# Retention and FFN in one kernel: w2's rows loaded ahead of the second pair of chunks, and the first tile's output blocks moved between those chunks' steps

## The chip, the cores and the metric

The kernel runs on one core of a Trainium2 chip. Its metric is the device time of one execution in microseconds (us). TensorE (PE) multiplies matrices into PSUM, VectorE (DVE), ScalarE (ACT) and GpSimd (POOL) do the elementwise work, and SyncE (SP) issues the DMAs that move data between HBM and SBUF. Each engine works through its own instructions in program order; semaphores order them among each other.

## The reference

Batch 4, 8 heads, 768 positions, head width 64; the FFN has 512 inputs and 1024 inner features. Inputs and output are float32.

```python
gamma = 1.0 - 2.0 ** (-5.0 - np.arange(H))
for t in range(S):
    state = gamma * state + outer(k[:, :, t], v[:, :, t])      # per batch and head, D x D
    y[:, :, t] = q[:, :, t] @ state / sqrt(D)
x = y.transpose(0, 2, 1, 3).reshape(B * S, H * D)              # 3072 x 512
out = (((x @ w1) * (x @ w2)) @ w3) @ w_out                     # 3072 x 512
```

## The kernel before

**Retention in chunks.** The sequence is cut into chunks of 128 positions, 6 for each of 4 batches, 24 in all. For chunk n the kernel casts q, k and v to 16 bits (v scaled by powers of gamma into the tile VP), transposes q and k, and then runs `scores(n)` (line 429: k times q into PSUM, masked by DVE into `am`, two operations at line 442), `kv(n)` (line 450: the update of the state; DVE adds at line 468 into `s`, POOL scales at line 469 into `t16`) and `outputs(n)` (line 472: v times `am` plus the state times q, and DVE scales the result into `XT` at line 485). `XT[m]` holds the transposed output of two chunks and is what the FFN reads.

**FFN by tiles.** w3 times w_out is multiplied once, at the start, into `W3O` (8 tiles). For each tile of up to 256 tokens an `a_unit` multiplies XT by w1 and ACT copies the result to `pa` (lines 515 to 518), a `b_unit` multiplies XT by w2 and DVE multiplies that with `pa` into `HT` (lines 520 to 527), and an `o_unit` multiplies 128 rows of HT by W3O, ACT evicts it with a scale, and SP stores it (lines 529 to 541). Tile 0 covers chunks 0 and 1, tile 1 chunk 2 alone, tile 2 chunk 3.

**The first tile is different.** Weights arrive by rows of 128, so `by_rows(W, ps, d)` (line 721) multiplies row block d of w1 or w2 into all eight output blocks, which fill four PSUM banks (`four_banks`, line 712). After four rows of w1 the banks are copied to SBUF (`pa`, held in two staging buffers), four rows of w2 follow, and DVE multiplies the two into `f0.HT` (lines 772 and 773). The rows are cast to 16 bits by ACT, DVE or POOL as they arrive.

**Chunks 0 to 3 are loaded in pairs** (`load_pair`, line 68): one DMA each for q, k and v of two chunks. In a pair's tiles half of each chunk lies on the wrong partitions, so `pair_casts` (line 303) is called twice for a chunk: once for the half that stays (POOL), once for the half that moves (DVE, or the engine that is named). It makes one cast of k, or two multiplications of v into VP, each over 64 partitions. `q_transposes(1, True)` transposes q of chunks 2 and 3 on PE and leaves the copies back to the caller (`q_back`). `transposes(n)` (line 406) transposes k on PE and writes two halves into KP, by ACT; for n = 2 DVE writes the second half (line 427).

**The order.** All of this is written out by hand: every engine runs its instructions in the order in which lines 645 to 779 call for them. The loads are issued at the start in the order of lines 133 to 145, on one queue, each into a free staging buffer; a DMA also waits for the eighth before it. From line 781 on a small queue of units (`fill`) feeds FFN work of tiles 1 and up between the steps of chunks 4 to 23 (`step`, line 600). In these steps `casts(n + 2)` (POOL), `dma_transposes(n + 2)` (line 385, two transposing DMAs on SP, from chunk 6 on) and `load_chunk(n + 4)` prepare the next chunks.

**Around the change.** Loads: row blocks of w1, then q and k of chunks 2 and 3, row 0 of w2, v, rows 1 to 3 of w2, then chunks 4 to 7. On PE, from line 730: rows 0 and 1 of w1, row 2, q transposes, part of row 3, k transposes of chunk 2, the rest of row 3, k transposes of chunk 3, scores(2), row 0 of w2, outputs(2), scores(3), row 1, kv(2), `a_unit(0)` of tile 1, row 2, `a_unit(2)`, row 3, `a_unit(4)`, outputs(3), `a_unit(6)`, kv(3), and the two output blocks of tile 0. The kernel is one function with nested helpers:

Of the kernel before, what the change touches and what calls it, by code (L numbers as in the profile page):

```python
# [12 lines left out]
MULT = mybir.AluOpType.mult  # L13
# [5 lines left out]
def kernel(  # L19
# [11 lines left out]
    nc = tc.nc  # L31
# [36 lines left out]
    def load_pair(m, names="qkv"):  # L68

        b, c = divmod(2 * m, NCH)  # L70
        for nm, src in (("q", q), ("k", k), ("v", v)):
            if nm not in names:
                continue
            if nm == "q":
                t = ld.tile([128, 2 * 512], FP, tag="q64", name="q64", bufs=3)
                q_in[m] = t
            else:
                t = new_stage()
                pair_in[nm, m] = t
            dma_in(  # L80
                t[:, :].rearrange("p (h x) -> p h x", x=2 * D),
                src[b, :, c * C : (c + 2) * C, :].rearrange("h (p t) d -> p h (t d)", t=2),
            )
# [26 lines left out]
    def load_rows(src, i):  # L110
        t = new_stage()
        dma_in(t[:, :], src[i * 128 : (i + 1) * 128, :])
        return t
# [23 lines left out]
    w3_st = {f: load_rows(moe_w3, f) for f in range(4, 8)}  # L137
    load_pair(0)
    w1_st = [load_rows(moe_w1, d) for d in range(4)]
    load_pair(1, "qk")  # L140
    w2_st = [load_rows(moe_w2, 0)]
    load_pair(1, "v")
    w2_st += [load_rows(moe_w2, d) for d in range(1, 4)]
    for n in range(4, 8):
        load_chunk(n)

# [64 lines left out]
    for h in range(H):  # L211
        p, r = h // 2, (h % 2) * 64
# [13 lines left out]
    def cast_to(dst, src, on_dve):  # L226
        if on_dve:
            nc.vector.tensor_copy(dst, src)  # L228
        else:
            nc.scalar.copy(dst, src)  # L230
# [72 lines left out]
    def pair_casts(n, moved, names="kv", eng=None):  # L303

        m, c = divmod(n, 2)
        rows = slice(c * 64, c * 64 + 64)
        t = 1 - c if moved else c
        to = slice(t * 64, t * 64 + 64)
        eng = eng or (nc.vector if moved else nc.gpsimd)
        if n not in k16s:  # L310
            k16s[n] = att.tile([128, 512], HP, tag="k16", name="k16", bufs=3)
        if "k" in names:
            (nc.scalar.copy if eng is nc.scalar else eng.tensor_copy)(
                k16s[n][to, :].rearrange("i (h d) -> i h d", d=D),
                pair_in["k", m][rows, :].rearrange("i (h t d) -> i h t d", t=2, d=D)[:, :, t, :],
            )
        for r in range(2 if "v" in names else 0):
            eng.tensor_tensor(  # L318
                VP[n % 3][to, :, r, r * 64 : r * 64 + 64],
                pair_in["v", m][rows, :].rearrange("j (p s t e) -> j p s t e", s=2, t=2, e=64)[:, :, r, t, :],  # L320
                VS2[rows, t, :].rearrange("j (p s) -> j p s", s=2)[:, :, r].unsqueeze(2).broadcast_to((64, NP, 64)),
                MULT,
            )
# [82 lines left out]
    def transposes(n, tag="psT"):  # L406
        if n >= NSTEP:
            return
        if by_dma(n):
            kT, kp = kTs.pop(n), KP[n % 2]  # L410
            nc.scalar.copy(kp[0:64, :, 0, :], kT[0:64, :, :])  # L411
            nc.scalar.copy(kp[64:128, :, 1, :], kT[64:128, :, :])  # L412
            return
        transposes_front(n, tag)
        transposes_back(n)

    def transposes_front(n, tag):
        k16 = k16s[n]
        ps = bank(tag, [128, NP, 128], HP, "psT")
        for p in range(NP):  # L420
            nc.tensor.transpose(ps[:, p, :], k16[:, p * 128 : (p + 1) * 128], ident16[:, :])
        kTs[n] = ps

    def transposes_back(n):
        kp, ps = KP[n % 2], kTs.pop(n)
        nc.scalar.copy(kp[0:64, :, 0, :], ps[0:64, :, :])
        cast_to(kp[64:128, :, 1, :], ps[64:128, :, :], n == 2)

    def scores(n, tags=("psA0", "psA1"), between=None):
        kp = KP[n % 2]  # L430
        am = att.tile([128, NP, 2, 128], HP, tag="am", name="am")
        for half in range(2):
            ps = bank(tags[half], [128, 2, 2, 128], FP, "psA")
            for i in range(2):
                p = half * 2 + i
                for r in range(2):
                    nc.tensor.matmul(  # L437
                        ps[:, i, r, :], lhsT=kp[:, p, r, :], rhs=queries(n, p), start=True, stop=True
                    )
            if half and between:  # L440
                between()
            nc.vector.tensor_tensor(  # L442
                am[:, half * 2 : half * 2 + 2, :, :].rearrange("j p s i -> j (p s) i"),
                ps[:, :, :, :].rearrange("j p s i -> j (p s) i"),
                (keep2 if n < 4 else keep)[:, :].unsqueeze(1).broadcast_to((128, 4, 128)),
                MULT,
            )
        ATs[n] = am

    def kv(n, tag="psK", eng=nc.gpsimd):  # L450
        k16, vp = k16s.pop(n), VP[n % 3]
        c = n % NCH
        if c == NCH - 1:
            return None
        ps = bank(tag, [128, NP, 128], FP, "psK")
        for p in range(NP):

            rhs = vp[:, p, :, :].rearrange("j s e -> j (s e)")
            rhs = bass.AP(rhs.tensor, rhs.offset, [list(rhs.ap[0]), [192, 2], [1, 64]])
            nc.tensor.matmul(  # L460
                ps[:, p, :], lhsT=k16[:, p * 128 : (p + 1) * 128], rhs=rhs, start=True, stop=True
            )
        t16 = att.tile([128, NP, 128], HP, tag="t16", name="t16")
        if c == 0:
            nc.vector.tensor_tensor(t16[:, :, :], ps[:, :, :], GS[:, :, :], MULT)
        else:
            s32 = att.tile([128, NP, 128], FP, tag="s32", name="s32")
            nc.vector.tensor_tensor(s32[:, :, :], ps[:, :, :], Tst[0][:, :, :], ADD)  # L468
            eng.tensor_tensor(t16[:, :, :], s32[:, :, :], GS[:, :, :], MULT)  # L469
        return t16  # L470
# [158 lines left out]
    def cast_w(W, st, d, on_dve):  # L629
        cast_to(W[d][:, :], st[d][:, :], on_dve)  # L630
# [81 lines left out]
    def four_banks(tags):  # L712
        got = []
        for t in tags:
            if t == "psF":
                got.append(ps_f.tile([128, 2, TB], FP, tag=t, name="psF"))
            else:
                got.append(bank(t, [128, 2, TB], FP, "psG"))
        return [t[:, :, :] for t in got]

    def by_rows(W, ps, d, cut=(0, TB), blocks=(0, 8)):
        cs = slice(*cut)
        for f in range(*blocks):
            nc.tensor.matmul(  # L724
                ps[f // 2][:, f % 2, cs], lhsT=W[d][:, f * 128 : (f + 1) * 128],
                rhs=XT[0][:, d, cs], start=(d == 0 and f % 2 == 0 and cut[0] == 0),
                stop=(d == 3 and f % 2 == 1),
            )
# [2 lines left out]
    by_rows(W1, ps, 0, (0, 128))  # L731
    by_rows(W1, ps, 0, (128, 256))
    by_rows(W1, ps, 1)
    for n in (2, 3):
        pair_casts(n, False, "k")
        pair_casts(n, True, "k", nc.scalar)
    by_rows(W1, ps, 2)
    q_back = q_transposes(1, True)
    q_back(0)
    q_back(1)  # L740
    by_rows(W1, ps, 3, blocks=(0, 3))
    transposes(2)
    by_rows(W1, ps, 3, blocks=(3, 8))
    transposes_front(3, "psK")
    pa = [hold[i // 2][:, i % 2 * 512 : i % 2 * 512 + 512].rearrange("p (a n) -> p a n", a=2) for i in range(4)]
    nc.gpsimd.tensor_copy(W2[0][:, :], w2_st[0][:, :])
    pair_casts(2, False, "v")
    pair_casts(3, False, "v")
    cast_to(pa[0], ps[0], False)
    cast_to(pa[1], ps[1], True)  # L750
    cast_to(pa[2], ps[2], False)
    scores(2, between=lambda: pair_casts(2, True, "v"))
    cast_to(pa[3], ps[3], True)
    transposes_back(3)
    cast_w(W2, w2_st, 1, False)
    cast_w(W2, w2_st, 2, False)
    cast_w(W2, w2_st, 3, False)
    ps = four_banks(("psF", "psF", "psF", "psT"))
    by_rows(W2, ps, 0)
    outputs(2, "psK")  # L760
    scores(3)
    by_rows(W2, ps, 1)
    t_new = kv(2, "psY")
    Tst[0] = t_new
    pair_casts(3, True, "v")
    f1 = ffn[1]
    f1.a_unit(0, "psK")
    by_rows(W2, ps, 2)
    f1.a_unit(2, "psA0")
    by_rows(W2, ps, 3)  # L770
    f1.a_unit(4, "psK")
    for i in range(4):
        nc.vector.tensor_tensor(f0.HT[:, 2 * i : 2 * i + 2, :], pa[i], ps[i], MULT)  # L773
    outputs(3, "psA1")
    f1.a_unit(6, "psA0")
    casts(4)
    Tst[0] = kv(3, "psK")
    f0.o_unit(0)
    f0.o_unit(1)

    for t in range(1, NT):
        late = ffn[t - 1].o_units() if t > 1 else []
# [49 lines left out]
```

## Time and profile before

| | us |
|---|---|
| median of 13 runs | 195.09 (194.71 to 196.02) |
| the profiled execution, its time | 195.44 |
| its span, first to last instruction | 193.5 |
| busy: PE / DVE / ACT / POOL | 184.4 / 117.9 / 99.3 / 85.4 |
| moved by DMA | 40.54 MB, 210 GB/s over the span |
| granted TensorE clock | 1.000 |

PE is busy for 95% of the span, so what matters is where it isn't: at the start, between 34 and 42 us, and at the end. In the rows of the profile each line gives the source line, the engine, the operation, the tile that is written and the tiles that are read; "L442 DVE ... am<-psA,keep" is the mask multiplication of the scores. In square brackets stands the time that the engine was idle before and the instruction or DMA that ended it. PEld is PE's weight load.

### The profile page before, as it was taken

What the parts mean: (1) busy time and instruction counts of PE and PEld (TensorE: products, weight loads), DVE (VectorE), ACT (ScalarE), POOL (GpSimd) and SP (SyncE); (2) the same over time, 40 slices, a digit from 0 to 9 for tenths busy, and PEclk for the clock granted to TensorE, in tenths of its full rate; (3) what the DMA queues carried; (4) which work ended last, traced back from release to release, by engine and by line L of the source; (5) the groups of instructions that cost most, each with busy time, mean ns of one, the idle gap of its engine ahead of it and who ended that gap; (6) DMA issues with size and microseconds to landing.
All of it is one profiled execution on the core that took longest, in us unless ns stands there. A gap on an engine that the chain in (4) does not pass through costs nothing.

```text
span 193.5 us, 4697 instructions
## 1 busy us (share of the span) xinstructions
PE 184.4 (95%) x1777; PEld 139.9 (72%) x1777; DVE 117.9 (61%) x220; ACT 99.3 (51%) x192; POOL 85.4 (44%) x146
## 2 busy tenths in 40 slices
PE   6799989879999999999999999999999999999993
PEld 2444657568797789777877787788778877887752
DVE  3227588599587768656665676575657665754220
ACT  6578455762445464455536453555455545533322
POOL 7600468638763747468152643862426432200000
PEclk9999999999999999999999999999999999999999
DMA  5999999998999989999999999969979931111004
GB/s 201 376 390 390 300 400 322 367 279 202 238 180 220 219 200 235 138 274 222 222 268 193 211 199 225 206 155 265 194 177 197 212 94 25 58 54 54 36 27 157
DMA packets 85030, 40.54 MB, mean 210 GB/s; under 512 B 61328, under 2 KB 80016, under 8 KB 85008
## 3 DMA queue, kind: packets, MB, share of 16 engines
q1 hardware_dynamic: 85008, 40.25, 87.9%
q8 instruction: 14, 0.23, 0.5%
q14 instruction: 8, 0.07, 0.2%
HBM read 29.36 MB, written 6.29 MB: 184 GB/s over the span
## 4 chain that ended last, share of the span: by engine, by line
PE 81%; DMA 10%; POOL 3%; DVE 2%; SPq 2%; issue 1%; ACT 1%; POOLq 0%; DVEq 0%
PE psF L508 39%; PE psO L534 21%; DMA stg<-in_v_dram 5%; PE psA L437 5%; DMA stg<-in_moe_w_dram 5%; PE psY L477 3%; PE psY L478 3%; PE psF L724 2%; PE psY L480 2%; PE psK L460 2%; POOL vp L318 2%; SPq L62 2%; PE psG L508 1%; PE psO L551 1%; DVE vp L318 1%
## 5 line engine op out<-in xcount | busy, mean ns | idle before, releaser
L508 PE MATMUL psF<-xt,w 128*128 128x256 f16 (+1 forms) x736 | 85.0, 266 | 0.0
L508 PEld LDWEIGHTS <-w 128*128 128x128 f16 x768 | 68.2, 98 | 7.2
L524 DVE TENSOR_TENSOR ht<-pa,psF 128x256 f16<-128x256 f32 x88 | 36.6, 417 | 22.5 <-PE psF L508 12.8
L518 ACT COPY pa<-psF 128x256 f32<-128x256 f32 x84 | 31.3, 372 | 33.8 <-PE psF L508 33.3
L442 DVE TENSOR_TENSOR am<-psA,keep 128x512 f16<-128x512 f32 x48 | 31.0, 685 | 21.0 <-PE psA L437 20.9
L534 PE MATMUL psO<-w3o,ht 128*128 128x512 f16 x184 | 43.3, 379 | 0.0
L469 POOL TENSOR_TENSOR t<-s,GS 128x512 f16<-128x512 f32 x15 | 19.3, 1284 | 37.5 <-DVE s L468 37.5
L539 ACT ACTIVATE osb<-psO 128x512 f32<-128x512 f32 x23 | 13.7, 597 | 37.0 <-PE psO L534 37.0
L534 PEld LDWEIGHTS <-ht 128*128 128x128 f16 x184 | 17.9, 98 | 16.9 <-DVE ht L773 0.2
L344 POOL TENSOR_TENSOR vp<-v,VS 128x256 f16<-128x256 f32 x40 | 23.8, 615 | 6.6 <-DMA v<-in_v_dram 2.5
L327 POOL CAST q<-q 128x1024 f16<-128x1024 f32 x12 | 12.6, 1053 | 27.3 <-DMA q<-in_q_dram 27.3
L485 DVE TENSOR_TENSOR xt<-psY,YS 128x512 f16<-128x512 f32 x24 | 17.8, 741 | 4.0 <-PE psY L480 3.6
L477 PE MATMUL psY<-am,vp 128*128 128x128 f16 x96 | 16.8, 219 | 1.0 <-POOL vp L318 0.8
L478 PE MATMUL psY<-am,vp 128*128 128x128 f16 x96 | 16.7, 219 | 0.6 <-DVE vp L318 0.6
L437 PEld LDWEIGHTS <-kp 128*128 128x128 f16 x192 | 12.5, 98 | 4.9 <-DVE kp L228 0.4
L340 POOL CAST k<-k 128x512 f16<-128x512 f32 x20 | 12.2, 611 | 5.2 <-PE psK L460 3.9
L468 DVE TENSOR_TENSOR s<-psK,t 128x512 f32<-128x512 f32 x16 | 11.0, 689 | 3.0 <-PE psK L460 2.7
L251 DVE COPY w3t<-psW 128x1024 f16<-128x1024 f16 x8 | 5.5, 690 | 10.0 <-PE psW L259 7.6
L437 PE MATMUL psA<-qTd,kp 128*128 128x128 f16 x144 | 11.1, 219 | 0.0
L411 ACT COPY kp<-kT 64x512 f16<-64x512 f16 x17 | 10.5, 618 | 0.8 <-DMA kT<-k 0.4
L480 PE MATMUL psY<-qTd,t 128*128 128x128 f16 x60 | 10.8, 219 | 0.0
L412 ACT COPY kp<-kT 64x512 f16<-64x512 f16 x17 | 10.5, 615 | 0.4
(82 smaller groups left out, 191.2 us busy)
## 6 DMA issues: line engine op xcount, KB each, us to landing
stg<-in_moe_w_dram SPq DMA_DIRECT2D x16, 512.0 KB, 8.3
q<-in_q_dram SPq DMA_DIRECT2D x12, 512.0 KB, 5.6
out_dram<-osb SPq DMA_DIRECT2D x23, 256.0 KB, 3.0
k<-in_k_dram SPq DMA_DIRECT2D x20, 256.0 KB, 5.3
v<-in_v_dram SPq DMA_DIRECT2D x20, 256.0 KB, 5.5
stg<-in_moe_w_out_dram SPq DMA_DIRECT2D x4, 512.0 KB, 7.2
stg<-in_k_dram SPq DMA_DIRECT2D x2, 512.0 KB, 11.0
stg<-in_v_dram SPq DMA_DIRECT2D x2, 512.0 KB, 8.5
```

Source lines behind the costliest of these rows:

```text
L344: nc.gpsimd.tensor_tensor(vp[:, :, r, r * 64 : r * 64 + 64], v32[:, :].rearrange("j (p s e) -> j p s e", s=2, e=64)[:, :, r, :], VS[:, :]. ...
L437: nc.tensor.matmul(ps[:, i, r, :], lhsT=kp[:, p, r, :], rhs=queries(n, p), start=True, stop=True)
L442: nc.vector.tensor_tensor(am[:, half * 2 : half * 2 + 2, :, :].rearrange("j p s i -> j (p s) i"), ps[:, :, :, :].rearrange("j p s i -> j ( ...
L469: eng.tensor_tensor(t16[:, :, :], s32[:, :, :], GS[:, :, :], MULT)
L477: nc.tensor.matmul(ps[:, p, :], lhsT=vp[:, p, 0, :], rhs=am[:, p, 0, :], start=True, stop=False)
L478: nc.tensor.matmul(ps[:, p, :], lhsT=vp[:, p, 1, :], rhs=am[:, p, 1, :], start=False, stop=(c == 0))
L480: nc.tensor.matmul(ps[:, p, :], lhsT=Tst[0][:, p, :], rhs=queries(n, p), start=False, stop=True)
L485: nc.vector.tensor_tensor(XT[n // 2][:, :, n % 2 * C : (n % 2 + 1) * C].rearrange("p a (i t) -> p a t i", t=2), ps[:, :, :].rearrange(orde ...
L508: nc.tensor.matmul(ps[:, i * w : (i + 1) * w], lhsT=W[d][:, (f + i) * 128 : (f + i + 1) * 128], rhs=XT[self.tok0 // TB][:, d, c0 : c0 + w] ...
L518: nc.scalar.copy(self.pa[f][:, :], ps[:, :])
L524: nc.vector.tensor_tensor(self.HT[:, f : f + TB // self.width, :].rearrange("p f n -> p (f n)"), self.pa.pop(f)[:, :], ps[:, :], MULT,)
L534: nc.tensor.matmul(psO[:, :], lhsT=self.HT[:, f, tb * 128 : (tb + 1) * 128], rhs=W3O[f][:, :], start=(f == 0), stop=(f == 7),)
```

## The change

The loads are reordered: all four rows of w2 come before the whole second pair. On PE the first tile now runs through: four rows of w1, four rows of w2, HT. The q transposes of chunks 2 and 3 follow, then the first output block of tile 0, the k transposes, and the second output block with scores(2) in its middle; then scores(3), kv(2), outputs(2), and the a units of tile 1 on PSUM banks of other names. The casts move along: w2's row 0 from POOL to ACT, row 3 from ACT to DVE; the moved half of v of chunk 2 goes ahead of its scores, that of chunk 3 ahead of scores(3). Instructions and their number on PE stay the same.

```diff
     load_pair(0)
     w1_st = [load_rows(moe_w1, d) for d in range(4)]
-    load_pair(1, "qk")
-    w2_st = [load_rows(moe_w2, 0)]
-    load_pair(1, "v")
-    w2_st += [load_rows(moe_w2, d) for d in range(1, 4)]
+    w2_st = [load_rows(moe_w2, d) for d in range(4)]
+    load_pair(1)
     for n in range(4, 8):
         load_chunk(n)
...
     by_rows(W1, ps, 1)
+    by_rows(W1, ps, 2)
+    by_rows(W1, ps, 3)
+    pa = [hold[i // 2][:, i % 2 * 512 : i % 2 * 512 + 512].rearrange("p (a n) -> p a n", a=2) for i in range(4)]
+    cast_w(W2, w2_st, 0, False)
+    cast_to(pa[0], ps[0], False)
+    cast_to(pa[1], ps[1], True)
+    cast_to(pa[2], ps[2], False)
+    cast_to(pa[3], ps[3], True)
+    cast_w(W2, w2_st, 1, False)
+    cast_w(W2, w2_st, 2, False)
+    cast_w(W2, w2_st, 3, True)
+    ps = four_banks(("psF", "psF", "psF", "psT"))
+    for d in range(4):
+        by_rows(W2, ps, d)
+    for i in range(4):
+        nc.vector.tensor_tensor(f0.HT[:, 2 * i : 2 * i + 2, :], pa[i], ps[i], MULT)
     for n in (2, 3):
         pair_casts(n, False, "k")
         pair_casts(n, True, "k", nc.scalar)
-    by_rows(W1, ps, 2)
     q_back = q_transposes(1, True)
     q_back(0)
     q_back(1)
-    by_rows(W1, ps, 3, blocks=(0, 3))
+    f0.o_unit(0)
     transposes(2)
-    by_rows(W1, ps, 3, blocks=(3, 8))
-    transposes_front(3, "psK")
-    pa = [hold[i // 2][:, i % 2 * 512 : i % 2 * 512 + 512].rearrange("p (a n) -> p a n", a=2) for i in range(4)]
-    nc.gpsimd.tensor_copy(W2[0][:, :], w2_st[0][:, :])
+    transposes(3, "psK")
     pair_casts(2, False, "v")
     pair_casts(3, False, "v")
-    cast_to(pa[0], ps[0], False)
-    cast_to(pa[1], ps[1], True)
-    cast_to(pa[2], ps[2], False)
-    scores(2, between=lambda: pair_casts(2, True, "v"))
-    cast_to(pa[3], ps[3], True)
-    transposes_back(3)
-    cast_w(W2, w2_st, 1, False)
-    cast_w(W2, w2_st, 2, False)
-    cast_w(W2, w2_st, 3, False)
-    ps = four_banks(("psF", "psF", "psF", "psT"))
-    by_rows(W2, ps, 0)
-    outputs(2, "psK")
-    scores(3)
-    by_rows(W2, ps, 1)
-    t_new = kv(2, "psY")
+    pair_casts(2, True, "v")
+    f0.o_unit(1, lambda: scores(2))
+    pair_casts(3, True, "v")
+    scores(3)
+    t_new = kv(2, "psY")
+    outputs(2, "psK")
     Tst[0] = t_new
-    pair_casts(3, True, "v")
     f1 = ffn[1]
-    f1.a_unit(0, "psK")
-    by_rows(W2, ps, 2)
-    f1.a_unit(2, "psA0")
-    by_rows(W2, ps, 3)
-    f1.a_unit(4, "psK")
-    for i in range(4):
-        nc.vector.tensor_tensor(f0.HT[:, 2 * i : 2 * i + 2, :], pa[i], ps[i], MULT)
+    f1.a_unit(0, "psT")
+    f1.a_unit(2)
+    f1.a_unit(4)
     outputs(3, "psA1")
     f1.a_unit(6, "psA0")
     casts(4)
     Tst[0] = kv(3, "psK")
-    f0.o_unit(0)
-    f0.o_unit(1)
```

## The prediction

> **What bounds the kernel now.** I read the page first: TensorE (PE) is busy for 95% of the span, and the DMA row shows the 16 DMA engines full until about 55 us.
>
> ```profile
> span 193.5 us, 4697 instructions
> PE 184.4 (95%) x1777; PEld 139.9 (72%) x1777; DVE 117.9 (61%) x220; ACT 99.3 (51%) x192; POOL 85.4 (44%) x146
> DMA  5999999998999989999999999969979931111004
> ```
>
> Then the busy times in two stretches: from the end of the third row of w1 (34.10) to the first matmul after the stage that the change rewrites (50.56), and from there to 180. After the span of the stretch come PE, PE's weight loads, DVE, ACT and POOL.
>
> ```profile
> 34.10:50.56 16.46, 14.17 (x154) 10.85 (x153) 13.41 (x21) 9.04 (x15) 10.27 (x13) 1.00 1.04 280
> 50.56:180.00 129.44, 129.44 (x1322) 105.27 (x1320) 83.45 (x161) 65.10 (x139) 59.11 (x80) 1.00 0.90 180
> ```
>
> After 50.56 PE is never idle. So whatever the stage gains or loses at 50.56 reaches the end whole; nothing behind it can swallow a delay. All that can be won lies in the first row. Busy time there includes the tails of single matmuls, so I count idle time by rate instead. In the chain of waits, eight 128-column matmuls take 0.45 us (0.055 each), sixteen of 512 columns 3.45 (0.216 each), and 256 columns take 0.11 each. From 34.10 to 50.56 the stage holds one row of w1 (0.88), four rows of w2 (3.52), the q transposes (0.44), the k transposes (0.44), two scores (0.88), two outputs (1.32), two state updates (0.44), four a units (1.76) and two output blocks (3.46): 13.14 us of work in 16.46, so **3.32 us idle**. PE's waits of 30 to 51 us name what it stands for, chunk 2's casts and scores:
>
> ```profile
> PE psY L477 <- POOL vp L318: 0.8, 1, 0.8
> PE psY L478 <- DVE vp L318: 0.6, 1, 0.6
> PE psT L421 <- POOL k L313: 0.5, 1, 0.5
> ```
>
> The timeline shows the pieces that I use below:
>
> ```profile
> 36.60 0.43 DVE L228 COPY kp<-psT 64x512 f16<-64x512 f16 x1 [1.08 <-ACT kp L426]
> ...
> 39.24 1.04 ACT L230 CAST w<-stg 128x1024 f16<-128x1024 f32 x1 [0.63 <-DMA stg<-in_moe_w_dram]
> ...
> 41.94 1.27 DVE L442 TENSOR_TENSOR am<-psA,keep 128x512 f16<-128x512 f32 x2
> ...
> 43.13 0.68 DVE L468 TENSOR_TENSOR s<-psK,t 128x512 f32<-128x512 f32 x1
> ...
> 43.96 1.44 POOL L469 TENSOR_TENSOR t<-s,GS 128x512 f16<-128x512 f32 x1 [3.48 <-DVE s L468]
> 44.19 1.49 DVE L318 TENSOR_TENSOR vp<-stg,VS 64x256 f16<-64x256 f32 x1
> ```
>
> **The loads.** Issue plus time to landing gives, before: last row of w1 31.1, q 33.0, k 34.7, row 0 of w2 36.0, v 37.7, rows 1 to 3 39.2, 40.5, 41.9. The engines are full, so I keep the bytes and exchange the order: a row costs about 1.3 us, q, k and v 1.8 each. After (estimate): rows of w2 at 32.4, 33.8, 35.1, 36.4; q 38.2, k 40.0, v 41.8. All later loads keep their place. SP is moved past nothing else: the output stores stay behind the load of v for chunk 7 (last issued at 50.36 before), and an earlier output block doesn't move them.
>
> **The stage after, step by step** (all estimates). Up to 34.10 nothing changes: w1's casts end at 32.5, and q's cast, the next on POOL, blocks nobody.
>
> 1. Row 3 of w1 runs 34.10 to 34.98, freed from waiting between transposes. ACT has cast w2's row 0 by 33.5. ACT evicts the first and third bank (0.58 each) to 35.1 and 35.7, DVE the others (0.69) to 35.4 and 36.1. w2's row 0 reuses three of these banks, so PE runs it at 35.16 to 36.18: 0.3 idle.
> 2. ACT then casts rows 1 and 2 (1.04 each): 36.74, 37.79. DVE casts row 3 (0.68, as `wo`'s cast by DVE) by 37.2. PE: row 1 36.79 to 37.67, row 2 37.84 to 38.72, row 3 to 39.60. Idle 0.8, for ACT.
> 3. q's cast on POOL (1.04) ends at 39.3, its transposes run 39.6 to 40.05. DVE multiplies HT in four pieces of 0.68 from 39.15: 39.83, 40.51, 41.19, 41.87. The first output block follows it: 40.05 to 42.35, idle 0.6. k's casts (0.61 each, two on POOL and two on ACT) are done at 41.3, hidden.
> 4. Both k transposes end at 42.8. ACT first evicts the output block (0.60) to 43.15, then writes its half of KP (0.58) to 43.73. DVE's half waits for ACT's, as in the row at 36.60, and ends at 44.2. It is the head of DVE's queue: v, am, v, am, s and XT stand behind it. PE has run half of the second output block and waits 0.5 for it; scores(2), the other half and scores(3) follow, with 0.6 idle for am buffers; state update and outputs(2) end at about 47.4.
> 5. From 44.2 DVE alone sets the pace: moved v of chunk 2 (2 x 0.42), am (1.28 a pair), moved v of chunk 3 (0.84), am (1.28), s (0.68), XT of chunk 2 (0.74): 5.66 us, so **49.86**. `a_unit(0)` of tile 1 reads that XT, and in program order nothing stands before it on PE: **2.4 us idle**. Before, XT of chunk 2 (41.31 to 42.06) was ready, with rows of w2 in front of the a units. The reserve of PE work has been spent early.
> 6. Three a units, outputs(3), the last a unit and kv(3) take 2.66 us: 52.5 instead of 50.56. Idle after: 0.3 + 0.8 + 0.6 + 0.5 + 0.6 + 2.4 = 5.2 against 3.3, so **+2.0 us**.
>
> **POOL's and SP's queues.** t of kv(2) (POOL, 1.44) now waits for s at 49.1; before it ran at 43.96. Behind it on POOL stand the casts of chunk 4, t of kv(3), then the casts of chunks 5 and 6. k of chunk 6 was cast by 54.0 and SP issued its DMA transpose at 54.03, q's at 55.37, landing 4.1 later at 59.5; scores(6) used it at 61.13, 1.6 us in reserve. After: t 49.1 to 50.5, q cast 51.6, k 52.2, v 53.4, t 54.7, chunk 5 56.5, q and k of chunk 6 at 58.2, so 4.2 late, where PE is 2.0 late. The reserve falls short by about 0.5 us: a new wait at scores(6). For chunk 8 the reserve of PE is larger by then (estimated transposes 74.2, use 75.2), and it ends there. Bounds: zero, if POOL's casts close up; 1.2, if ACT's KP copies, which wait for the same DMA, hold up the pa copies behind them. I take 0.5. Total **+2.5**.
>
> [...] The row at 44.19 shows a moved v of 1.49 us beside a POOL multiply; the one just ahead of it, begun with POOL idle, took 0.42. [...] Here POOL's four v operations (0.61 each from 41.85) end at 44.3, just as DVE starts, so I take 0.42; if v came 1.5 us later, chunk 2's pair would cost 1.62 (as at 38.38) and the total would grow by 0.8. [...] The granted clock is 1.00 in both rows above, across a longest wait of 0.8. By the row the gap costs only its 2.4[...]. At 2.4 I take nothing and keep 1.7 for the upper end.
>
> **How it could go otherwise.**
> - *The forecast*, chance 0.62: DVE's backlog ahead of XT, +1.7 to +3.0, at +2.5. For: from 44.2 each operation is at about the shortest duration the trace has, so the backlog can hardly shrink.
> - *The arrival gap goes and the backlog stays covered*: faster. The place is the wait of `a_unit(0)`. If it were nought, the rest of the idle is 2.8 against 3.3, so -0.5; with KP not held behind the output block's eviction, up to -1.6. It decides when XT of chunk 2 ends before 47.9, two us ahead of my sum, as it would if the trace's DVE times contain waits that the new order lacks. Median 193.5 to 194.6, some 194.2. Against: DVE's queue order. Chance 0.08, and 0.04 for no change between.
> - *The moved loads come later than the bytes say*: v after 43.5, so POOL and DVE collide and DVE starts late: +3.3, 198.4 in the median. For: 512-byte pieces were issued slowly here (3.2 to 3.9 us of SP for one k). Against: landings were paced by the full engines. Chance 0.16.
> - *The gap grows to a clock drop, or POOL's lag lasts beyond chunk 6*: +4.2, 199.3. Chance 0.10.
>
> **The numbers.** The profiled execution took 195.44 us, 193.5 of them span and 1.9 around it; the sum gives 195.44 + 2.5 = 197.9. The median of the 13 runs is 0.35 lower: 195.09 + 2.5 = **197.6**. The range 196.1 to 199.3 leaves out the faster case and the tail of the last. Within 0.2% (0.4 us, about what a measurement can tell from no change) 0.04, faster 0.08, slower 0.88.
>
> **What would show it.** In the changed profile: last row of w2 landed by 37 and v near 42; PE dense between 36.8 and 39.6; the longest wait of PE, above 1.5 us, at the first a unit of tile 1 (before line 508) for DVE's XT; DVE without a gap from 44 to 50; the first b unit of tile 1 at 52 to 53; a short wait of scores(6) for the transposed q; no idle PE from then on. I am wrong if that a unit waits under 0.5 us, if a wait for a DMA leads in this stage, or if the b unit starts at 52.5 and the end doesn't move.

## The result, and the profile after

| | before | changed |
|---|---|---|
| median, us | 195.02 (48 runs, 194.69 to 196.24) | **199.05** (11 runs, 197.31 to 199.63) |
| ratio | 1 | **1.0187**, 95% interval 1.0168 to 1.0206 |
| profiled execution: time / span | 195.44 / 193.5 | 198.91 / 196.6 |
| granted clock, mean over the span | 1.000 | 0.991 |

The changed kernel is 4.0 us slower. Its executions fall into two groups: with the profiled one there are twelve, three of them at 197.3 to 197.4 with a mean clock of 0.998, and nine at 198.9 to 199.6 with 0.990 or 0.991. Of the 4.0 us some 0.3 lie outside the span (time less span is 2.2 us in the median, 1.9 for the kernel before). From the profile's page after the change:

```profile
span 196.6 us, 4691 instructions
PE 186.4 (95%) x1777; PEld 141.0 (72%) x1777; DVE 116.7 (59%) x221; ACT 99.4 (51%) x192; POOL 83.6 (43%) x145
...
PEclk9999999999699999999999999999999999999999
```

The share of busy PE is the same 95%, but in the eleventh slice (49 to 54 us) stands a 6: TensorE's clock was lowered there. The stretch from the end of w1's third row to the first b unit of tile 1, and the rest:

```profile
34.10:53.64 19.54, 16.71 (x158) 12.34 (x156) 11.36 (x21) 8.06 (x15) 8.59 (x12) 0.91 1.16 257
53.64:183.00 129.36, 129.36 (x1323) 105.20 (x1321) 84.04 (x163) 64.87 (x139) 60.19 (x80) 1.00 0.87 173
```

The b unit came at 53.64 and not at 50.56, 3.1 later, and the span is 3.1 longer. In this execution the third row of w1 ended at 34.39 and not at 34.10, so 0.3 of the 3.1 lie ahead of the stage; the stage itself took 19.25 us for the 13.14 us of PE work that took 16.46 before. The second row shows PE without a gap from there to 183 us, as before to 180: the loss went through one to one. PE's waits (30 to 54 us) have changed their kind; the three waits for casts of chunk 2 that led the list are gone, and one wait for DVE's XT has taken their place:

```profile
PE psG L506 <- DVE xt L483: 2.1, 1, 2.1
PE psA L435 <- DVE kp L226: 0.2, 1, 0.2
PE psA L435 <- DVE am L440: 0.2, 1, 0.2
PE psF L722 <- ACT w L228: 0.2, 1, 0.2
```

DVE's timeline ahead of it (start, duration):

```profile
43.51 0.43 DVE L226 COPY kp<-psT 64x512 f16<-64x512 f16 x1 [1.13 <-ACT kp L424]
43.86 0.75 DVE L316 TENSOR_TENSOR vp<-stg,VS 64x256 f16<-64x256 f32 x2
44.64 1.29 DVE L440 TENSOR_TENSOR am<-psA,keep 128x512 f16<-128x512 f32 x2
45.96 0.76 DVE L316 TENSOR_TENSOR vp<-stg,VS 64x256 f16<-64x256 f32 x2
46.75 1.29 DVE L440 TENSOR_TENSOR am<-psA,keep 128x512 f16<-128x512 f32 x2
47.96 0.68 DVE L466 TENSOR_TENSOR s<-psK,t 128x512 f32<-128x512 f32 x1
48.55 0.72 DVE L483 TENSOR_TENSOR xt<-psY,YS 128x512 f16<-128x512 f32 x1
```

No gap from 43.51 to 49.27: DVE is the bound of this stretch, and chunk 3's v and am (2.1 us) stand ahead of chunk 2's XT. At 49.33 PE's a unit starts. Then the second loss: three windows of 3.41 us, counted from the instant at which the trace shows the clock going down.

```profile
46.37:49.78 3.41, 1.33 (x25) 1.22 (x23) 2.88 (x6) 0.00 (x0) 1.00 (x1) 1.00 1.13 254
49.78:53.19 3.41, 3.41 (x36) 3.41 (x34) 0.20 (x1) 1.12 (x3) 2.96 (x5) 0.50 1.26 230
53.19:56.60 3.41, 3.41 (x61) 3.28 (x60) 3.09 (x8) 1.53 (x3) 1.92 (x3) 1.00 0.42 139
```

PE was busy for 1.33 of 3.41 us in the first; in the second it ran at a granted clock of 0.50, which costs half of 3.41, 1.7 us (1.7 of 196.6 is the 0.009 that the mean clock of 0.991 lacks). So the 3.1 us are 1.7 from the clock, 1.1 of more idle PE in the stage and 0.3 ahead of it.

### The profile page after: what moved, and what is told of

It reads as the page before. It is cut to its first block, busy times and chain, and to the rows that moved or that the text cites. A ratio compares the mean times of both kernels' runs of the same rounds, so it can differ in the third digit from the quotient of the medians.

```text
span 196.6 us, 4691 instructions
## 1 busy us (share of the span) xinstructions
PE 186.4 (95%) x1777; PEld 141.0 (72%) x1777; DVE 116.7 (59%) x221; ACT 99.4 (51%) x192; POOL 83.6 (43%) x145
## 4 chain that ended last, share of the span: by engine, by line
PE 81%; DVE 8%; DMA 5%; ACT 2%; SPq 1%; issue 1%; ACTq 0%
PE psF L506 39%; PE psO L532 20%; DMA stg<-in_moe_w_dram 5%; PE psA L435 5%; PE psY L476 2%; PE psY L475 2%; DVE am L440 2%; PE psF L722 2%; PE psY L478 2%; PE psK L458 2%; SPq L62 1%; DVE vp L316 1%; PE psW L291 1%; DVE xt L483 1%; PE psO L549 1%
## 5 line engine op out<-in xcount | busy, mean ns | idle before, releaser
L506 PE MATMUL psF<-xt,w 128*128 128x256 f16 (+1 forms) x752 | 86.9, 267 | 0.0
L506 PEld LDWEIGHTS <-w 128*128 128x128 f16 x768 | 69.0, 99 | 9.1 <-issue 2.2
L516 ACT COPY pa<-psF 128x256 f32<-128x256 f32 x86 | 32.0, 372 | 34.6 <-PE psF L506 34.2
L532 PE MATMUL psO<-w3o,ht 128*128 128x512 f16 x184 | 44.1, 379 | 0.0
L475 PE MATMUL psY<-am,vp 128*128 128x128 f16 x96 | 17.2, 223 | 0.0
L476 PE MATMUL psY<-am,vp 128*128 128x128 f16 x96 | 17.2, 223 | 0.0
```

The source lines that it names most:

```text
L475: nc.tensor.matmul(ps[:, p, :], lhsT=vp[:, p, 0, :], rhs=am[:, p, 0, :], start=True, stop=False)
L476: nc.tensor.matmul(ps[:, p, :], lhsT=vp[:, p, 1, :], rhs=am[:, p, 1, :], start=False, stop=(c == 0))
L506: nc.tensor.matmul(ps[:, i * w : (i + 1) * w], lhsT=W[d][:, (f + i) * 128 : (f + i + 1) * 128], rhs=XT[self.tok0 // TB][:, d, c0 : c0 + w] ...
L516: nc.scalar.copy(self.pa[f][:, :], ps[:, :])
L532: nc.tensor.matmul(psO[:, :], lhsT=self.HT[:, f, tb * 128 : (tb + 1) * 128], rhs=W3O[f][:, :], start=(f == 0), stop=(f == 7),)
```

## The experiments

The theory to be tested: DVE's queue ahead of XT costs the changed kernel some 2 us, and the gap that it opens on PE lowers the clock, which costs 1.7 more in most executions. The rivals: the clock has another reason; the later loads of q, k and v are the cost. Each kernel was timed beside runs of the kernel before on the same chip (medians 195.1 to 195.2).

**e1, PE kept busy in the gap.** The changed kernel, and

```diff
     f1 = ffn[1]
+    psZ = ps_t.tile([128, 512], FP, tag="psT", name="psZ")
+    for _ in range(8):
+        nc.tensor.matmul(psZ[:, :], lhsT=W1[0][:, 0:128], rhs=W1[0][:, 0:512], start=True, stop=True)
     f1.a_unit(0, "psT")
```

> The changed kernel with 8 matmuls of 512 columns (0.216 us each, 1.73 together) put on PE just before the first a unit of tile 1, where PE waits 2.1 us for DVE's XT; nothing reads their result, and they need no data that is late. My theory (the wait opens a gap in which PE's clock falls to half for 3.4 us, 1.7 us of delay, in most executions): the added work fits in the gap, no drop, about 197.3 in every run, the XT wait shrunk to some 0.4 and PE's next matmul at the same time 49.3. Rival one (the clock falls for another reason, or the two groups of times at 197.3 and 199.1 are chance): times still in two groups, median 199. Rival two (PE's work itself is the bound there): slower by 1.7, about 200.8.

Measured 197.48 (197.25 to 198.69, 6 runs), ratio 1.0119 (1.0079 to 1.0159), clock 1.000 in every run. PE's longest wait in this stage is now

```profile
PE psG L506 <- DVE xt L483: 0.3, 1, 0.3
```

Eight matmuls of work more, and 1.6 us less. So the clock drop comes from the gap, and it is worth about the 1.7 that the half clock made of 3.41 us. What is left, 2.4 us over the kernel before, agrees with the changed kernel's three executions without a drop (2.3); this run doesn't take it apart.

**e2, less work ahead of XT on DVE.**

```diff
-    pair_casts(3, True, "v")
+    pair_casts(3, True, "v", nc.gpsimd)
```

> The changed kernel with only the moved half of v of chunk 3 taken from DVE (0.76 us for two) to POOL, which is idle from 44.0 to 48.8. My theory (DVE's backlog ahead of XT of chunk 2 sets the first a unit of tile 1): XT 0.76 earlier, PE's wait 2.1 to 1.3, first b unit 0.8 earlier; 196.5 without a clock drop, and with a gap of only 1.3 the drop should be gone in most runs, so median 196.5 to 197. Rival (PE is held by the later loads, not by DVE's queue): no change, 199 in the median, since no load moves. If POOL's longer queue (q cast of chunk 4 onwards) matters, less than 0.8 is won.

Measured 197.32 (196.58 to 197.91, 8 runs), ratio 1.0096 (1.0064 to 1.0127), no drop in any run. The wait for XT was 1.2. But the median is that of the changed kernel's executions without a drop (197.3): all of the gain is the clock's, and the expected 0.76 was not won. With six v operations on POOL, DVE's own pair for chunk 2 took 1.49 beside them and not 0.75:

```profile
41.59 3.96 POOL L316 TENSOR_TENSOR vp<-stg,VS 64x256 f16<-64x256 f32 x6 [0.50 <-DMA stg<-in_v_dram]
43.59 1.49 DVE L316 TENSOR_TENSOR vp<-stg,VS 64x256 f16<-64x256 f32 x2
```

From the end of DVE's half of KP to the end of XT it is 5.16 us here and 5.33 in the changed kernel, so 0.2 shorter; PE waited 0.9 for `am` instead. The rival with the loads is not settled by this run; it is by e7 and e10, which keep these loads and are 4.4 and 3.1 us faster than the changed kernel.

**e3, XT of chunk 2 ahead of chunk 3.**

```diff
-    pair_casts(3, True, "v")
-    scores(3)
     t_new = kv(2, "psY")
     outputs(2, "psK")
     Tst[0] = t_new
+    pair_casts(3, True, "v")
+    scores(3)
```

> The changed kernel with kv(2) and outputs(2) called before the moved v and the scores of chunk 3, so that s and XT of chunk 2 stand ahead of v and am of chunk 3 (0.76 + 1.29 us) in DVE's queue. Theory (DVE's queue order is the cause): XT of chunk 2 ends at about 47.5 in place of 49.3, scores(3) runs in the rest of the gap, a units from 47.6; then XT of chunk 3 becomes what PE waits for, outputs(3) needs am of chunk 3 at about 49.7. First b unit at 51.2 to 51.6 (52.1 without drop before this edit), time 196.2 to 196.8, no clock drop. Rival (late loads): no change, 199.

Measured 198.27 (197.02 to 199.62, 6 runs), ratio 1.0161 (1.0114 to 1.0209); three runs with the drop; the three without (197.0 to 197.9) are no faster than the changed kernel's. My expectation was too good. XT did end early, at 47.36, and PE's wait for it fell to 0.4. But DVE's timeline shows what then came, and POOL's what ran beside it:

```profile
47.40 2.11 DVE L316 TENSOR_TENSOR vp<-stg,VS 64x256 f16<-64x256 f32 x2
49.54 1.29 DVE L440 TENSOR_TENSOR am<-psA,keep 128x512 f16<-128x512 f32 x2
```

```profile
46.79 1.27 POOL L467 TENSOR_TENSOR t<-s,GS 128x512 f16<-128x512 f32 x1 [2.68 <-DVE s L466]
48.00 1.24 POOL L325 CAST q<-q 128x1024 f16<-128x1024 f32 x1
```

The moved v of chunk 3 took 2.11 in place of 0.76, because it now lies beside POOL's multiply and q cast (which itself took 1.24 in place of 1.04). PE's wait went to am of chunk 3, 2.0 us. The queue's order was right, the place of v was not.

**e4 and e5, half of the change each.** e4 is the changed kernel with the loads as before; e5 the kernel before with the new loads.

```diff
-    w2_st = [load_rows(moe_w2, d) for d in range(4)]
-    load_pair(1)
+    load_pair(1, "qk")
+    w2_st = [load_rows(moe_w2, 0)]
+    load_pair(1, "v")
+    w2_st += [load_rows(moe_w2, d) for d in range(1, 4)]
```

> The changed kernel with the loads in the order of before: q and k of chunks 2 and 3, row 0 of w2, v, rows 1 to 3. Theory (the new PE order needs w2 early; the later arrival of q, k, v is hidden): rows 1 to 3 of w2 land at 39.2, 40.5, 41.9, the fourth row runs 42.6 to 43.5 in place of 39.6, everything behind is 3.9 later: 201 without a clock drop, up to 204 with one or two drops in the longer waits. Rival (the delay of q, k and v by 4 to 5 us is what costs the change its 2 to 4 us): with these loads the kernel returns to 195 to 197.

> The kernel before with the new order of the loads alone. Theory (the old PE order needs q and k of chunk 2 early, the new one doesn't; each half of the change needs the other): the q transposes stand behind the third row of w1 and wait for q, which lands at about 37.8 in place of 33.0, k at 39.7 in place of 34.7; PE idles some 4 to 5 us from 34.1, part of it is won back since w2 is then there: first b unit 3 to 4 later[...]: 199 to 201. Rival (the load order costs nothing by itself): 195.

Measured: e4 203.92 (203.71 to 204.22, 4 runs), ratio 1.0438 (1.0393 to 1.0482), clock 0.975 in all; e5 200.73 (200.51 to 202.10, 4 runs), ratio 1.0291 (1.0236 to 1.0345). Each half alone is worse than both together, so load order and PE order belong together. The 199 to 201 for e5 counts one clock drop of the changed kernel's size, 1.7 us (estimate). In e5 PE waits 5.1 us in one piece for q's cast; PE was busy for 0.00 us of the window from 35.78 to 39.19, and the mean clock of the run is 0.991 (0.981 to 0.983 in the other three). In e4 two waits for ACT, which itself stands waiting for rows of w2, come on top of the wait for XT (e5, then e4):

```profile
PE psTq L364 <- POOL q L325: 5.1, 1, 5.1
```

```profile
PE psF L724 <- ACT stg L230: 2.5, 1, 2.5
PE psG L508 <- DVE xt L485: 2.1, 1, 2.1
PE psF L724 <- ACT w L230: 1.0, 1, 1.0
```

**e6, the head of DVE's queue earlier.**

```diff
-    f0.o_unit(0)
-    transposes(2)
+    f0.o_unit(0, lambda: transposes(2, "psY"))
```

> The changed kernel with the k transposes of chunk 2 put in the middle of the first output block (on another bank), so that ACT writes its half of KP ahead of that block's eviction and DVE's half, the head of its queue, ends at about 42.6 in place of 43.9. If step 4 of the prediction (the wait for ACT's half) sets the start of DVE's backlog fully, XT comes 1.2 earlier and the time is 196.1 without a clock drop. [...]DVE's moved v of chunk 2 then falls beside POOL's four v operations (41.5 to 44.0) and takes about 1.5 in place of 0.75: XT only 0.3 to 0.5 earlier, gap still about 1.7, time 197.0 without and 198.7 with the clock drop. I expect the second.

Measured 198.06 (196.49 to 198.53, 6 runs), ratio 1.0122 (1.0081 to 1.0164); five runs with the drop, the one without at 196.49. In its profile DVE's half of KP ends at 42.66, 1.3 earlier, but v of chunk 2 takes 1.33 beside POOL, and XT ends at 48.58, 0.7 earlier. Of both, 0.2 was there at the third row of w1 (34.20 against 34.39), so XT gained 0.5, as expected for the longer v.

**e7, all three.** The early k transposes, XT of chunk 2 first, and v of chunk 3 on POOL ahead of everything that POOL does for the state:

```diff
-    f0.o_unit(0)
-    transposes(2)
+    f0.o_unit(0, lambda: transposes(2, "psY"))
     transposes(3, "psK")
     pair_casts(2, False, "v")
     pair_casts(3, False, "v")
     pair_casts(2, True, "v")
+    pair_casts(3, True, "v", nc.gpsimd)
     f0.o_unit(1, lambda: scores(2))
-    pair_casts(3, True, "v")
-    scores(3)
     t_new = kv(2, "psY")
     outputs(2, "psK")
     Tst[0] = t_new
+    scores(3)
```

> The changed kernel with three edits at once: early k transposes of chunk 2 as in e6, moved v of chunk 3 on POOL as in e2 but ahead of its multiply for the state, and kv(2) and outputs(2) ahead of scores(3) as in e3. Theory (DVE's queue ahead of XT is the whole of the loss): DVE does v, am, s, XT of chunk 2 in a row, XT ends at about 47.0, a units from 47.1, am of chunk 3 at 48.4, outputs(3) right behind the a units; first b unit at about 49.9, 0.7 before that of the kernel before: 194.3, no clock drop in any run. [...]

Measured 194.68 (194.03 to 195.47, 20 runs), ratio 0.9970 (0.9954 to 0.9985): faster than the kernel before, and clear of the 195.5 to 196.5 that were expected if a slower v beside POOL (1.49 in e2) or POOL's longer queue took the gain back. The waits of PE in this stage:

```profile
PE psG L506 <- DVE xt L483: 0.4, 1, 0.4
PE psF L722 <- ACT w L228: 0.2, 1, 0.2
```

XT ends at 46.6, the first b unit starts at 49.34, 1.2 before that of the kernel before, and no run has the drop. The time is only 0.5 better: 0.3 is lost outside the span, as in the changed kernel, and the two profiled executions lie some 0.2 off their kernels' median spans, to opposite sides. The loads and the order of the first tile on PE are those of the changed kernel, so what cost it the 4 us was the order in DVE's and POOL's queues and the clock drop that follows from it.

**e8 and e9, a cast on an idle engine.** e8 adds to e7

```diff
-    cast_w(W2, w2_st, 1, False)
+    nc.gpsimd.tensor_copy(W2[1][:, :], w2_st[1][:, :])
```

> As e7, and row 1 of w2 cast by POOL, which is idle from 33 to 38, in place of ACT, so that the pass over w2 no longer waits for ACT's casts in turn (0.8 us of idle PE by step 2 of the prediction). If the pass over w2 sets the start of what follows: HT and the output blocks 0.7 earlier, up to 193.5. If the landing of k (39.7) and v (41.4) sets it: no more than 0.2 against e7.

Measured 198.69 (197.44 to 199.81, 6 runs), ratio 1.0163 (1.0120 to 1.0206), five runs with the drop. I had looked at POOL's idle time and not at its queue:

```profile
37.98 1.04 POOL L325 CAST q<-q 128x1024 f16<-128x1024 f32 x1 [5.83 <-DMA q<-in_q_dram]
38.96 1.04 POOL L740 CAST w<-stg 128x1024 f16<-128x1024 f32 x1
```

q's cast is called earlier in the program and waits 5.8 us for its DMA; the new cast stood behind it, and PE waited 3.2 us for row 1. e9 calls `q_cast(1)` after that cast:

> As the run before it, with the cast of q of chunks 2 and 3 called after row 1's cast, so that POOL no longer waits for q's landing (37.8) ahead of it. The pass over w2 then ends at about 38.9 in place of 39.5 and PE does not wait for ACT's casts. Theory (what follows hangs on k at 39.7 and v at 41.4): the k transposes still run at 41.0, no more than 0.2 against e7, 194.5. Rival (the pass over w2 sets the rest): 0.6 less than e7, 194.1.

Measured 194.11 (193.25 to 195.39, 22 runs), ratio **0.9936** (0.9917 to 0.9955), the fastest version. XT's 0.4 is the only wait listed for PE between 30 and 54 us. It is 0.6 below e7, half of it within the span. Its profiled execution was late from the start (third row of w1 at 34.97, e7's at 34.30); counted from there DVE begins HT 0.43 sooner and the first b unit comes 0.56 sooner than in e7. So the pass over w2 does set what follows, as far as one trace of each can tell, and my bound by the landings of k and v was wrong.

**e10, e7 without the early k transposes.**

> e7 without the early k transposes: only the moved v of chunk 3 on POOL and kv(2), outputs(2) ahead of scores(3). Theory (DVE's queue ahead of XT is the loss[...]): DVE starts v of chunk 2 at 43.7 and takes 1.5 beside POOL, am 45.1 to 46.4, s and XT to 47.8, a units from 47.8 in place of 46.7 in e7: 195.4 to 195.8, no clock drop. If the two reorderings alone carried the gain, 194.7.

Measured 195.91 (195.05 to 196.93, 22 runs), ratio 1.0023 (1.0002 to 1.0044). As expected, slightly above: v of chunk 2 took 1.48 beside POOL. XT ended at 48.6, in an execution whose third row of w1 ended 0.7 later than e7's. So of e7's 4.4 us against the changed kernel some 3.1 belong to the two reorderings, with the clock drop, and 1.0 to 1.2 (by ratios or by medians) to the early transposes.

## Why the prediction was right, and where it fell short

The sign held, and so did the mechanism up to the gap: DVE's backlog leaves PE waiting for XT. That 199.05 lies in the range, near its upper end, is in part luck: the forecast of 197.6 is 1.4 too low, and errors of both signs stand behind it.

| | forecast, us | measured, us |
|---|---|---|
| more idle PE in the stage (steps 1 to 6) | 2.0 | 1.1 (e1: 1.3) |
| POOL's and SP's queues | 0.5 | 0 |
| clock drop | 0 | 1.7 |
| ahead of the stage and outside the span | 0 | 1.2, what remains of the 4.0 |

- *Loads:* right within 0.4 us. Landings were 32.2, 33.5, 34.8, 36.1 for w2's rows, 37.8, 39.7, 41.4 for q, k, v (forecast 32.4 to 36.4; 38.2, 40.0, 41.8). One reading was wrong: the DMA row stays at 8 or 9 with hardly a break until about 155 us, not 55. No term rests on the 55.
- *Steps 1 to 3:* the pass over w2 ended at 39.6, as forecast; the output block could follow HT as described.
- *Step 4:* DVE's half of KP waited for ACT's (the 1.13 in the row above) and ended at 43.9; forecast 44.2.
- *Step 5:* DVE's seven rows run without a gap, XT at 49.27; forecast 49.86. PE waited 2.1, forecast 2.4.
- *Step 6:* right in kind, too large in size. The stage's 19.25 us less the 1.7 of the clock and 13.14 of work leave 4.4 idle, where 5.2 were forecast and 3.3 stood before: +1.1 and not +2.0. Without the clock's 1.7 the first b unit would have come at 51.9; forecast 52.5. The executions without a drop are 2.3 above the kernel before, near the forecast, but only because of the last line of the table: 0.3 is time outside the span, and in the profile 0.3 came ahead of the third row of w1. The sum put nothing there; where the rest arose was not found.
- *POOL's and SP's queues, +0.5:* wrong. No wait of scores(6) appears, in the changed kernel or in e1. POOL was as late as forecast (e1: SP issued the transpose of k of chunk 6 at 57.98; its cast was forecast for 58.2), but in the changed kernel's trace the transposing DMAs then landed 2.5 and 3.2 us after issue, against 4.0 and 4.1 before. The DMA share over that time was 0.52 (59.22 to 63.78) against 0.88 (54.03 to 59.5): SP had waited 8.0 us for POOL's cast (2.0 before) and issued nothing meanwhile. I had carried over a time to landing from a stretch with a DMA share of 0.88 to one with 0.52.
- *"At 2.4 I take nothing":* this is the term that was mis-sized: it measured 1.7 in nine of twelve executions. The 1.7 kept for the upper end was my estimate: the clock of the profile before is 1.000 over its whole span and shows no drop. I took it that only a gap longer than 2.4 us could bring one, which no row showed; in the changed kernel's trace the clock went to 0.50 after a wait of 2.1 us, with PE busy for 1.33 of the 3.41 us ahead of the drop. The rival "the gap grows to a clock drop", 199.3, named the right event and nearly the right time with a chance of 0.10, and with a condition (a longer gap) that was not needed.
- *The rival on the other side* was the right shape: in e7 and e9, with XT of chunk 2 at 46.6 and 46.7, ahead of the 47.9 that was named, the reordered kernel is faster, by 0.5 and 1.1 us (0.5 to 1.6 were forecast). It needed another order on DVE, which the change didn't have.

## What to carry to other kernels

When PE work is moved forward to cover late data, ask what then stands in front of the next consumer on the engine that feeds it: here PE's spare rows were spent early, and a DVE queue with another chunk's work ahead of one XT was left bare. Where a hole on PE is as long as the one here (2.1 us of waiting, PE busy for 1.33 of 3.41 us), look at the granted clock behind it: the hole counted twice in the changed kernel, once for its length and once for the 1.7 us that the half clock after it took. Before work is given to an idle engine, read what its queue is waiting for (5.8 us for q's DMA on POOL in e8), and what the engine beside it does at that time (DVE's pair of v took 1.49 us beside POOL's six v operations in e2, 0.75 in the changed kernel).

## What the runs showed of the hardware

**The clock went down after windows in which PE was busy for 0.00 to 1.34 of 3.41 us.** In the clock record of the changed kernel's trace the stretch at full begins at 5.41 us and ends at 49.78, 13 times 3.413 later; then the clock is 0.50 for 3.413 us and full again for 143.36, 42 times 3.413. Taking windows of 3.41 us in such steps on each trace, the drop followed those in which PE was busy for 0.00 (e5), 0.92 and 1.34 (e4) and 1.33 us (changed). It did not follow 1.64 (e8's profile, 38.29 to 41.70), 1.74 (e6's) or 1.82 (before); the rows of the last two:

```profile
46.96:50.37 3.41, 1.74 (x32) 1.74 (x32) 1.62 (x3) 0.95 (x3) 2.28 (x3) 1.00 1.11 253
```

```profile
36.89:40.31 3.42, 1.82 (x19) 1.38 (x20) 3.33 (x6) 2.75 (x5) 2.77 (x5) 1.00 1.04 385
```

So in these traces a window at full clock with PE busy for 1.34 us or less (39%) was followed by a drop, and one with 1.64 (48%) or more was not; what lies between was not seen. In e4 the clock was at 0.50 through a window in which PE was busy for 2.40 us and through the next, in which it was busy for all of 3.42, and came back after that.

The steps don't begin with the kernel: the stretch at full begins at 6.18 us in the trace before, at 5.41 in the changed kernel's, and between 4.2 and 7.6 in the traces here. If each step counts by itself, the same gap of 2.1 us can lie in one window in some executions and across two in others. That is my reading of the two groups of times, as far as the traces can tell. I let the steps begin at every point over each trace, from 20 to 60 us. In the changed kernel's trace 46% of the beginnings give a window under 1.34 us and 63% one under 1.64; nine of twelve executions had the drop. In the traces of e1, e2, e7, e9 and e10 no window holds less than 1.66, and none of their 78 executions had it. Two things stay open: where the windows lay in the executions without a trace was not seen, and the kernel before, whose trace has no window under 1.77, had a drop in 4 of the 81 executions timed beside the experiments (196.9 to 197.5 us, mean clock 0.990 or 0.991).

**Operations of DVE and POOL took longer beside each other.** A pair of DVE's multiplications of v took 0.75 or 0.76 us in the changed kernel and in e8, with POOL idle for all or nearly all of it, and 1.17 to 2.11 beside POOL's multiplications and casts (e9 1.17, e7 1.29, e6 1.33, e10 1.48, e2 1.49, e3 2.11). POOL's cast of q took 1.24 in place of 1.04 beside DVE's pair in e3. Moving one pair from DVE to POOL (e2) took 0.76 off DVE's queue and put 0.74 back, because the other pair grew. What makes them take longer was not shown.
